# When weight pieces are converted in a fused attention and expert kernel, a third buffer of queries and keys, and when constant rows are written

## The chip, the cores and the metric

The kernel runs on one core of a Trainium2 chip. The metric is the device time of one execution in microseconds (us), given as the median of several runs.

## The reference

Three layers follow each other, all in float32; N = 2304 tokens (4 batches of 576), width 512.

```python
scores = 0.125 * q @ k.T           # 8 heads of 64; heads 0-3 a local mask of 32, heads 4-7 a strided one
attn = softmax(where(mask, scores, -1e9))
x = (attn @ v) -> (N, 512)
h = maximum(maximum(x @ w1, x @ w2), x @ w3)      # 512 -> 768
x = h @ w_out                                     # 768 -> 512
logits = x @ w_gate + modality_bias[modality_id]  # 8 experts, the largest logit chooses one
out[t] = gate[t] * (relu(x[t] @ w1[e]) @ w2[e])   # e = e(t); 512 -> 1024 -> 512
```

The weights w1, w2, w3 and w_out arrive as 64-bit words, and the kernel itself makes float32 of them.

## The kernel before

TensorE works on tokens in blocks of 384 (`TB`), six in all. For each block the function `L1(j, f)` computes the three products with w1, w2, w3 for one of six slices of 128 columns: three steps (m = 0, 1, 2) of 12 matmuls each, so 18 steps for a block. Each product is made of three matmuls, since every operand is held as a high and a low part. In the step with m = 0 ScalarE copies the bank of PSUM out, in the other two VectorE takes the maximum (L513). `L2(j)` is the product with w_out in six steps of 18 matmuls. A step takes the next bank by `mm_bank()`, which turns over two banks for as long as weights are being converted, and three later.

Attention is cut into 40 groups (batch, pair of heads, part), in the order of `order(b)`. One call of `slot()` is one slot: when it *ticks*, attention moves by one group through a pipeline of six stages (S of group t, maximum of t-1, exponential of t-2, reciprocal and product of t-3, transposition of t-4, product with v and its copy out of t-5). The matmul part of a slot ("rest", in `later`) is put out by `flush()`, in the middle of the next step of 12 matmuls. Ahead of block 0 stand 13 slots (t = 0 to 12) with no L1 step in them: there each slot is followed by four matmuls on constant data (`keep_warm(4)`, L861). I call these 13 slots the opening. After it, block 0's steps k = 1 to 18 each end in a slot; of these the odd ones up to 15 tick.

Conversion of a weight piece (24 pieces of 512 KB, 18 for w1 to w3 and 6 for w_out) also goes by slots, when `slot` is called with `conv`. It runs over three slots: `conv_abs` (ScalarE, L366), four VectorE operations of `conv_ops` (L378, L381, L383, L385, each needs the one before), and `conv_split` (ScalarE L397, POOL L398). Three stage buffers hold raw pieces, and the load of a further piece is asked for by `load_piece` right behind L385. The six pieces of w_out are followed by a transposition (`gate_T`, L405), which takes a bank by `mm_bank` as well, and a small product (`gate_G`, L411). Before, the opening converts from slot 4 on (`CS = 4`): nine of 13 slots. Block 0 converts in `pieces = 10 + 12 * k // 16`, so in all steps but k = 5, 9, 13 and 17; block 1 does what is left.

All loads stand in one queue, that of SP (SyncE), in the order of the program; one that waits holds up all behind it. Queries and keys of a pair of heads (608 KB) lie in one of two buffers, `qk_b[p % 2]`, and are asked for two slots ahead of the group that needs them (`load_qk(t + 2)`, L192). The scratch rows `xs`, into which POOL scatters the tokens by expert, are first filled with ones by eight DMAs from the tile `filler` (L902), in the steps k = 17 and 18 of block 0 and 1 to 6 of block 1. `L2(0)` stands behind five of the six slices of block 1. The outputs of L1 (`h_of`) lie in a ring of 11 chunks. The wide tile `y` is the buffer of three of four pieces in conversion; its first 72 columns hold the modality ids before that, from which POOL makes the bias table `ball` (L877 to L879) behind slot 1.

Of the kernel before, what the change touches and what calls it, by code (L numbers as in the profile page):

```python
# [106 lines left out]
def tile_attention_moe_moe(ctx: ExitStack, tc: tile.TileContext, qk, vw, w, wg, ids, bias, e12, cst, out):  # L107
# [7 lines left out]
    HT = sb.tile([128, 4608], F32R, name="HT")  # L115
    HX = sb.tile([128, 3072], F32R, name="HX")
    stage = sb.tile([128, 3, 2, 512], F32, name="stage")
# [24 lines left out]
    def f32(ap):  # L142
        return ap.bitcast(F32)
# [10 lines left out]
    spare = R[:, xo + 2 * KD * XR:xo + 2 * KD * XR + 768]  # L154
    chunks = [z[:, 768 * i:768 * i + 768] for z, n in ((HT, 6), (HX, 4)) for i in range(n)] + [spare]

    def h_of(j, f):
        return chunks[(NF * j + f) % 11].rearrange("p (s t) -> p s t", s=2)

    ht = [HT[:, 768 * i:768 * i + 768].rearrange("p (s t) -> p s t", s=2) for i in range(6)]  # L160
    ht2 = ht + [W[:, 16384 + 768 * i:16384 + 768 * i + 768].rearrange("p (s t) -> p s t", s=2) for i in range(2)]
    at_pool = tc.tile_pool(name="at", bufs=1)
    AT = at_pool.__enter__().tile([128, 5504], F32, name="AT")
    qk_b = [AT[:, 1216 * i:1216 * i + 1216].rearrange("p (s n) -> p s n", s=2) for i in range(2)]
    v_b = [AT[:, 2432 + 384 * i:2432 + 384 * i + 384].rearrange("p (c d) -> p c d", c=3) for i in range(3)]
    s_b = [AT[:, 3584 + 384 * i:3584 + 384 * i + 384] for i in range(3)]
    pt_b = [AT[:, 4736 + 384 * i:4736 + 384 * i + 384].rearrange("p (c q) -> p c q", c=3) for i in range(2)]

# [4 lines left out]

    filler = sb.tile([128, ROW // 2], F32R, name="filler")

# [11 lines left out]
    st = {}  # L187

    def load_qk(i):
        if i < NG and groups[i][2] == 0:  # L190
            b, p, _ = groups[i]
            SP.dma_start(qk_b[p % 2], qk[b, p])  # L192

# [31 lines left out]
    def att_S(i):  # L225
        b, p, g = groups[i]
        us, _ = units(p, g)
        t = qk_b[p % 2]
        ps, _, _, n, w_ = s_view(i)
# [121 lines left out]
    def load_piece():  # L351
        i = step["load"]
        if i < NW:
            step["load"] += 1
            SP.dma_start(stage[:, i % 3].rearrange("p a n -> p (a n)").bitcast(I32),
                         w[i].bitcast(I32))
# [63 lines left out]
    DEPTH = 5  # L420
    CS, FILL = 4, 16
    later, delayed, next_slot = [], [], []
# [5 lines left out]
    def slot(ticks=True, conv=True):  # L428
# [31 lines left out]
        def rest():  # L460
# [12 lines left out]
            if ticks:  # L473
                if t >= 2:
                    load_v(t - 2)
                if t:
                    load_qk(t + 2)

# [368 lines left out]
    with tc.manual_schedule():  # L847
# [15 lines left out]
        DVE.memset(t1s, 0.0)  # L863
        POOL.memset(AT[:, 3584:4736], 0.0)
        keep_warm(9)
        POOL.memset(f32(filler), 1.0)
        for t in range(LEAD + DEPTH):
            slot(conv=t >= CS)
            flush()
            keep_warm(4)  # L870
            if t == 1:
# [7 lines left out]
                POOL.tensor_tensor(out=ball, in0=ball, in1=other, op=ALU.add)  # L879
            if t == 2:  # L880
                for _ in range(3):
                    load_piece()

# [6 lines left out]
        for j in range(NB):  # L890
            parts = [(L1, j, f) for f in range(NF)]
            if j:
                parts.insert(NF - 1 if j == 1 else 1, (L2, j - 1))
            n = sum(3 if p_[0] is L1 else 2 * NS for p_ in parts) - 2
            start = now[0]
            k = 0
            for fn, *arg in parts:
                for _ in fn(*arg):
                    k += 1
                    if FILL <= fills < FILL + E:  # L900
                        e_ = fills - FILL
                        SP.dma_start(xs[NT * e_:NT * e_ + TB].rearrange("(p s) (h n) -> p (s h) n", p=128, h=2),  # L902
                                     f32(filler)[:, None, :].to_broadcast([128, 2 * NS, ROW // 2]))
                    fills += 1
                    due = goal.get(j, start)
                    pieces = 10 + 12 * k // 16 if j == 0 else NW + 3
                    slot(now[0] < min(due, start - (start - due) * k // n), fn is L1 and step["conv"] < pieces)
# [63 lines left out]
```

## Time and profile before

| | us |
|---|---|
| median of 3 runs | 640.86 |
| lowest, highest | 639.35, 643.72 |
| profiled execution, whole | 642.5 |
| its span from the first to the last instruction | 640.7 |
| outside the span | 1.8 |

The profile is of one execution. Its busy times and waits are those of the span; a time of a row counts from the span's start.

### The profile page before, as it was taken

The page shows a single profiled execution, that of the slowest core. Times are in us where ns is not written, and L with a number is a line of the kernel's source. Part 1 is how long each engine was busy: PE and PEld are TensorE (multiplying, and loading weights), DVE is VectorE, ACT ScalarE, POOL GpSimd, SP SyncE. Part 2 cuts the span into 40 slices and gives each one's busy share as a digit, 9 for nine tenths or more (in the row PEclk, how much of TensorE's full clock was granted, in tenths as well). Part 3 has the DMA queues.
Part 4 walks back from the last instruction along what each step waited for, and adds up shares of the span by engine and source line. Part 5 has one row for each costly group of instructions (what it writes and reads, how often), then busy time and mean ns, then how long its engine had stood idle before and what let it go on. Part 6 is the DMA issues. An engine that isn't in the chain of part 4 may idle for free. (4 is left out here: it accounts for less than half of the span.)

```text
span 640.7 us, 11895 instructions
## 1 busy us (share of the span) xinstructions
PE 612.7 (96%) x4597; PEld 563.6 (88%) x4603; DVE 258.2 (40%) x701; ACT 230.2 (36%) x695; POOL 136.1 (21%) x157
## 2 busy tenths in 40 slices
PE   7889998999999999999999999999999999999992
PEld 4558987899999999999999999998998979898981
DVE  4987996322334432442131123275344215331210
ACT  2868664333243334333211111352344124322220
POOL 2444553212131321032113103101102010111010
PEclk9979999999999999999999999999999999999997
DMA  6676459991022312020000004244442127220201
GB/s 229 228 274 211 160 189 234 178 161 44 22 74 63 108 55 65 23 78 10 10 18 34 1 1 145 86 134 136 160 133 86 47 75 243 83 67 33 68 19 40
DMA packets 30669, 64.45 MB, mean 101 GB/s; under 512 B 3328, under 2 KB 14336, under 8 KB 30592
## 3 DMA queue, kind: packets, MB, share of 16 engines
q1 hardware_dynamic: 27712, 54.01, 29.5%
q0 software_dynamic: 2880, 9.46, 3.9%
q8 instruction: 43, 0.70, 0.5%
q14 instruction: 34, 0.28, 0.1%
HBM read 47.68 MB, written 15.77 MB: 99 GB/s over the span
## 5 line engine op out<-in xcount | busy, mean ns | idle before, releaser
L494 PE MATMUL bank<-R,W 128*128 128x384 f32 (+1 forms) x1350 | 253.3, 343 | 3.3 <-DVE t1s L513 2.0
L494 PEld LDWEIGHTS bank<-R,W 128*128 128x128 f32 x1350 | 235.8, 188 | 9.5 <-DVE t1s L513 3.0
L494 PE MATMUL bank<-R,HT 128*128 128x260 f32 (+1 forms) x540 | 89.9, 316 | 0.3 <-POOL HT L505 0.3
L513 DVE TENSOR_TENSOR t1s<-bank,t1s 128x384 f32<-128x384 f32 x72 | 40.1, 557 | 122.5 <-PE bank L494 121.4
L494 PEld LDWEIGHTS bank<-R,HT 128*128 128x128 f32 x540 | 78.0, 188 | 6.8 <-POOL HT L505 0.5
L719 POOL DMA_INDIRECT out_dram<-y,gi x18 | 18.0, 1000 | 155.8 <-ACT x2h L700 99.0
L494 PE MATMUL bank<-x2h,R 128*128 128x384 f32 x192 | 49.5, 336 | 1.1 <-ACTq L927 1.1
L277 POOL TENSOR_TENSOR AT<-AT,mx 128x288 f32<-128x288 f32 (+2 forms) x40 | 27.1, 677 | 110.2 <-DVE mx L273 103.5
L494 PE MATMUL bank<-x2h,W 128*128 128x384 f32 x192 | 49.8, 337 | 0.0
L711 DVE SCALAR_TENSOR_TENSOR HT<-bank,HT 128x384 fp32r<-128x384 f32 x36 | 20.1, 557 | 63.1 <-ACT HT L710 62.9
L262 ACT ACTIVATE AT<-bank,mx 128x96 f32<-128x96 f32 (+1 forms) x138 | 43.1, 334 | 2.5 <-DVE R L415 1.7
L718 ACT ACTIVATE y<-bank,gi 128x512 f32<-128x512 f32 x18 | 12.4, 690 | 76.5 <-PE bank L494 63.1
L494 PE MATMUL bank<-W,HT 128*128 128x512 f32 x162 | 38.5, 391 | 0.0
L505 POOL TENSOR_TENSOR HT<-t1s,HT 128x384 fp32r<-128x384 f32 x21 | 21.3, 1014 | 73.5 <-ACT HT L504 73.4
L236 PE MATMUL bank<-AT 64*64 64x54 f32 (+1 forms) x640 | 32.0, 240 | 5.1 <-DMA AT<-in_qk_dram 4.4
L494 PEld LDWEIGHTS bank<-x2h,R 128*128 128x128 f32 x192 | 34.7, 188 | 1.6 <-ACTq L927 1.5
L494 PEld LDWEIGHTS bank<-W,HT 128*128 128x128 f32 x162 | 30.1, 188 | 6.0
L494 PEld LDWEIGHTS bank<-x2h,W 128*128 128x128 f32 x192 | 34.8, 188 | 0.3 <-issue 0.3
L236 PEld LDWEIGHTS bank<-AT 64*64 64x64 f32 x640 | 25.3, 139 | 11.1 <-DMA AT<-in_qk_dram 5.2
L710 ACT ACTIVATE HT<-bank 128x384 fp32r<-128x384 f32 x36 | 17.7, 492 | 47.0 <-PE bank L494 39.0
L343 DVE TENSOR_TENSOR R<-bank,R 128x162 fp32r<-128x162 f32 (+2 forms) x56 | 20.7, 397 | 32.3 <-ACT R L339 32.3
L511 ACT COPY t1s<-bank 128x384 f32<-128x384 f32 x36 | 17.3, 480 | 43.8 <-PE bank L494 39.0
(158 smaller groups left out, 803.3 us busy)
## 6 DMA issues: line engine op xcount, KB each, us to landing
stage<-in_w_dram SPq DMA_DIRECT2D x24, 512.0 KB, 4.2
stage<-in_e_dram SPq DMA_DIRECT2D x48, 256.0 KB, 3.3
AT<-in_qk_dram SPq DMA_DIRECT2D x15, 608.0 KB, 5.5
xs<-filler SPq DMA_DIRECT2D x8, 771.0 KB, 16.9
rows<-xs SPq DMA_DIRECT2D x7, 771.0 KB, 4.7
AT<-in_vw_dram SPq DMA_DIRECT2D x24, 144.0 KB, 3.6
AT<-in_vw_dram SPq DMA_DIRECT2D x16, 192.0 KB, 3.5
AT<-in_qk_dram SPq DMA_DIRECT2D x1, 352.0 KB, 5.2
```

The costliest lines, as they stand in the source:

```text
L236: PE.matmul(ps[r, c], lhsT=t[r, 0, q0:q0 + 64], rhs=t[r, 1, q0:q0 + w_], start=not pe, stop=True, skip_group_check=pe)
L262: ACT.activation(out=s3[:, c], in_=ps[:, c], func=AF.Exp, scale=0.125, bias=m[1][:, c:c + 1], accum_out=m[2][:, c:c + 1])
L277: POOL.tensor_tensor(out=s3, in0=s3, in1=m[3][:, :, None].to_broadcast([128, n, w_]), op=ALU.mult)
L343: DVE.tensor_tensor(out=l, in0=src, in1=f32(h), op=ALU.subtract)
L494: PE.matmul(ps, lhsT=a, rhs=b_, start=i == 0, stop=i == n - 1)
L505: POOL.tensor_tensor(out=h[:, 1], in0=t1, in1=f32(h[:, 0]), op=ALU.subtract)
L511: ACT.copy(t1, ps)
L513: DVE.tensor_tensor(out=t1, in0=ps, in1=t1, op=ALU.max)
L710: ACT.activation(out=h[:, 0], in_=ps, func=AF.Relu)
L711: DVE.scalar_tensor_tensor(out=h[:, 1], in0=ps, scalar=0.0, in1=f32(h[:, 0]), op0=ALU.max, op1=ALU.subtract)
L718: ACT.activation(out=y[:, s, :DM], in_=ps, func=AF.Copy, scale=gi[:, s, 0:1])
L719: POOL.indirect_dma_start(out=out[:, :], out_offset=bass.IndirectOffsetOnAxis(ap=gi[:, s, 1:2].bitcast(I32), axis=0), in_=y[:, s, :DM], in ...
```

## The change

Conversion begins at slot 2 of the opening and ends there with slot 8 (seven slots, pieces 0 to 6 begun), then goes on in each of the first 15 steps of block 0, pauses in steps 16 to 18 and finishes in block 1. The first three pieces are asked for behind slots 0, 1 and 2, one each. Queries and keys get a third buffer and are asked for three slots ahead. The eight fills start when the last piece has been asked for, one in every second step, each with rows of 514 elements where it had half rows of 257. `L2(0)` stands behind three slices of block 1, and the ring of chunks has 9.

```diff
-    HX = sb.tile([128, 3072], F32R, name="HX")
+    HX = sb.tile([128, 1536], F32R, name="HX")
...
-        return chunks[(NF * j + f) % 11].rearrange("p (s t) -> p s t", s=2)
+        return chunks[(NF * j + f) % 9].rearrange("p (s t) -> p s t", s=2)
...
-    AT = at_pool.__enter__().tile([128, 5504], F32, name="AT")
-    qk_b = [AT[:, 1216 * i:1216 * i + 1216].rearrange("p (s n) -> p s n", s=2) for i in range(2)]
+    AT = at_pool.__enter__().tile([128, 6720], F32, name="AT")
+    qk_b = [AT[:, 1216 * i:1216 * i + 1216].rearrange("p (s n) -> p s n", s=2) for i in range(3)]
...
-    filler = sb.tile([128, ROW // 2], F32R, name="filler")
+    filler = sb.tile([128, ROW], F32R, name="filler")
...
+    def qk_of(b, p):
+        return qk_b[(4 * b + (p + 2) % 4) % 3]
...
-            SP.dma_start(qk_b[p % 2], qk[b, p])
+            SP.dma_start(qk_of(b, p), qk[b, p])
...
-    CS, FILL = 4, 16
+    CS, AHEAD = 2, 7
...
-                    load_qk(t + 2)
+                    load_qk(t + 3)
...
-            slot(conv=t >= CS)
+            slot(conv=CS <= t < CS + AHEAD)
...
-            if t == 2:
-                for _ in range(3):
-                    load_piece()
+            if t < 3:
+                load_piece()
...
-                parts.insert(NF - 1 if j == 1 else 1, (L2, j - 1))
+                parts.insert(3 if j == 1 else 1, (L2, j - 1))
...
-                    if FILL <= fills < FILL + E:
-                        e_ = fills - FILL
-                        SP.dma_start(xs[NT * e_:NT * e_ + TB].rearrange("(p s) (h n) -> p (s h) n", p=128, h=2),
-                                     f32(filler)[:, None, :].to_broadcast([128, 2 * NS, ROW // 2]))
-                    fills += 1
+                    if step["load"] == NW and fills < 2 * E:
+                        if fills % 2 == 0:
+                            e_ = fills // 2
+                            SP.dma_start(xs[NT * e_:NT * e_ + TB].rearrange("(p s) n -> p s n", p=128),
+                                         f32(filler)[:, None, :].to_broadcast([128, NS, ROW]))
+                        fills += 1
...
-                    pieces = 10 + 12 * k // 16 if j == 0 else NW + 3
+                    pieces = min(AHEAD + k, 22) if j == 0 else NW + 3
```

VectorE in slots 9 and 10 of the opening, before. The mx rows and L244 are attention's, L378 to L385 are one piece in conversion, L343 is the copy out of an attention group.

```order
L269 TENSOR_SCALAR mx<-mx 128x3
L378 TENSOR_SCALAR y<-y 128x512
L273 RECIPROCAL mx<-mx 128x3
L381 TENSOR_SCALAR bank_82<-y 128x512
L244 TENSOR_REDUCE bank_83<-bank_83 128x3
L383 SCALAR_TENSOR_TENSOR bank_82<-stage,bank_82 128x512
L254 TENSOR_SCALAR mx<-bank_83 128x3
L385 SCALAR_TENSOR_TENSOR y<-stage,bank_82 128x512
L343 TENSOR_TENSOR R<-bank_86,R 128x192
```

The same place now; lines of the changed kernel are higher by three.

```order
L272 TENSOR_SCALAR mx<-mx 128x3
L276 RECIPROCAL mx<-mx 128x3
L247 TENSOR_REDUCE bank_83<-bank_83 128x3
L257 TENSOR_SCALAR mx<-bank_83 128x3
L346 TENSOR_TENSOR R<-bank_86,R 128x192
```

So the four operations of a piece have gone from there, as from slots 11 and 12; two of these four pieces now stand in slots 3 and 4, one more is in block 0 and one more in block 1.

VectorE in step 5 of block 0, before: a step that ticks, with no piece in it. L513 is the maximum of an L1 step.

```order
L513 TENSOR_TENSOR t1s<-bank_81,t1s 128x384
L269 TENSOR_SCALAR mx<-mx 128x6
L273 RECIPROCAL mx<-mx 128x6
L244 TENSOR_REDUCE bank_83<-bank_83 128x3
L254 TENSOR_SCALAR mx<-bank_83 128x3
L343 TENSOR_TENSOR R<-bank_86,R 128x9x18
L343 TENSOR_TENSOR R<-bank_87,R 128x9x18
L513 TENSOR_TENSOR t1s<-bank_80,t1s 128x384
```

The same step now.

```order
L516 TENSOR_TENSOR t1s<-bank_81,t1s 128x384
L272 TENSOR_SCALAR mx<-mx 128x6
L381 TENSOR_SCALAR y<-y 128x512
L276 RECIPROCAL mx<-mx 128x6
L384 TENSOR_SCALAR bank_82<-y 128x512
L247 TENSOR_REDUCE bank_83<-bank_83 128x3
L386 SCALAR_TENSOR_TENSOR bank_82<-stage,bank_82 128x512
L257 TENSOR_SCALAR mx<-bank_83 128x3
L388 SCALAR_TENSOR_TENSOR y<-stage,bank_82 128x512
L346 TENSOR_TENSOR R<-bank_86,R 128x9x18
L346 TENSOR_TENSOR R<-bank_87,R 128x9x18
L516 TENSOR_TENSOR t1s<-bank_80,t1s 128x384
```

A piece has come in between the two maxima, here and in steps 9 and 13; steps 16 and 18 have lost theirs.

SP's queue before, from the fifth weight piece asked for: `stage` is a weight piece, `AT` from `in_qk_dram` a load of queries and keys, from `in_vw_dram` one of values.

```order
L355 DMA stage<-in_w_dram 128x1024
L198 DMA AT<-in_vw_dram 96x384
L355 DMA stage<-in_w_dram 128x1024
L198 DMA AT<-in_vw_dram 96x384
L355 DMA stage<-in_w_dram 128x1024
L198 DMA AT<-in_vw_dram 96x384
L192 DMA AT<-in_qk_dram 128x1216
```

Now, from the seventh piece on:

```order
L358 DMA stage<-in_w_dram 128x1024
L201 DMA AT<-in_vw_dram 96x384
L358 DMA stage<-in_w_dram 128x1024
L201 DMA AT<-in_vw_dram 96x384
L195 DMA AT<-in_qk_dram 128x1216
L358 DMA stage<-in_w_dram 128x1024
L201 DMA AT<-in_vw_dram 96x384 x2
L195 DMA AT<-in_qk_dram 128x1216
```

The two loads of queries and keys at the end, for groups 10 and 12, stand one slot earlier, and behind the second the pieces of the slots 9 to 12 are gone.

## Rows read from the trace of the kernel before

**Rows 1.** The page's first part: busy time of each engine, share of span, instructions.

```profile
PE 612.7 (96%) x4597; PEld 563.6 (88%) x4603; DVE 258.2 (40%) x701; ACT 230.2 (36%) x695; POOL 136.1 (21%) x157
```

**Rows 2.** Timeline, TensorE, opening: start, duration, count, [idle before <- releaser].

```profile
28.52 1.04 PE L861 MATMUL bank<-t1s 128*128 128x512 bf16 x4
29.39 0.49 PE L286 MATMUL bank<-cs,AT 128*96 128x128 f32 x3
30.42 0.57 PE L313 MATMUL bank<-AT 96*64 96x64 f32 x12 [0.54 <-DVE R L343]
30.92 0.30 PE L232 MATMUL bank<-cs 128*128 128x288 bf16 x1
31.14 0.71 PE L236 MATMUL bank<-AT 64*64 64x96 f32 x12
...
36.53 1.53 PE L236 MATMUL bank<-AT 64*64 64x54 f32 x24 [2.28 <-DMA AT<-in_qk_dram]
...
46.27 3.52 PE L494 MATMUL bank<-R,W 128*128 128x384 f32 x18
```

**Rows 3.** Timeline, VectorE, opening: where slots 3, 6 and 9 begin.

```profile
10.85 0.49 DVE L268 TENSOR_REDUCE mx<-AT 128x6 f32<-128x324 f32 x1 [0.18 <-ACT AT L259]
...
19.77 0.42 DVE L268 TENSOR_REDUCE mx<-AT 128x5 f32<-128x270 f32 x1
...
30.49 0.16 DVE L269 TENSOR_SCALAR mx<-mx 128x3 f32<-128x3 f32 x1
```

**Rows 4.** Stretches: length, busy of each engine (instructions), granted clock, DMA share, GB/s.

```profile
10.85:19.77 8.92, 8.59 (x121) 5.58 (x122) 7.56 (x21) 4.25 (x15) 2.27 (x4) 1.00 1.00 360
36.00:41.00 5.00, 4.47 (x41) 2.95 (x43) 3.84 (x10) 2.70 (x10) 2.86 (x3) 0.50 0.91 305
46.30:92.80 46.50, 46.36 (x432) 42.27 (x430) 39.73 (x90) 32.26 (x114) 23.13 (x22) 1.00 0.59 194
```

**Rows 5.** Timeline, TensorE, end of block 0: waits for a bank.

```profile
93.70 0.66 PE L405 MATMUL bank<-cs,y 128*128 128x128 f32 x4 [0.86 <-DVE t1s L513]
...
97.89 1.31 PE L494 MATMUL bank<-R,W 128*128 128x384 f32 x6 [0.62 <-ACT t1s L511]
...
102.26 3.44 PE L494 MATMUL bank<-R,W 128*128 128x384 f32 x18 [0.72 <-DVE t1s L513]
```

**Rows 6.** Timeline, VectorE, block 0, steps 6 to 15.

```profile
65.27 0.56 DVE L513 TENSOR_TENSOR t1s<-bank,t1s 128x384 f32<-128x384 f32 x1 [0.55 <-PE bank L494]
...
68.59 0.16 DVE L269 TENSOR_SCALAR mx<-mx 128x5 f32<-128x5 f32 x1
...
72.03 0.54 DVE L513 TENSOR_TENSOR t1s<-bank,t1s 128x384 f32<-128x384 f32 x1
72.50 0.41 DVE L378 TENSOR_SCALAR y<-y 128x512 f32<-128x512 f32 x1
...
75.47 0.16 DVE L269 TENSOR_SCALAR mx<-mx 128x3 f32<-128x3 f32 x1
...
77.11 0.92 DVE L378 TENSOR_SCALAR w<-w 128x512 f32<-128x512 f32 x1
...
84.00 0.56 DVE L513 TENSOR_TENSOR t1s<-bank,t1s 128x384 f32<-128x384 f32 x1
...
89.71 0.56 DVE L513 TENSOR_TENSOR t1s<-bank,t1s 128x384 f32<-128x384 f32 x1 [1.08 <-PE bank L494]
...
93.09 0.55 DVE L513 TENSOR_TENSOR t1s<-bank,t1s 128x384 f32<-128x384 f32 x1
```

**Rows 7.** Timelines, POOL and ScalarE, opening: last bias operation, first Abs.

```profile
10.54 0.49 POOL L879 TENSOR_TENSOR ball<-ball,rt 128x144 f32<-128x144 f32 x1
...
14.91 0.67 ACT L366 ACTIVATE y<-stage 128x512 f32<-128x512 f32 x1 [1.30 <-DMA stage<-in_w_dram]
```

**Rows 8.** Timeline, SP: issue of the load that group 10 waits for.

```profile
30.93 0.42 SPq L192 DMA_DIRECT2D AT<-in_qk_dram  x1
```

**Rows 9.** Timeline, POOL, block 0: an operation that runs beside a piece's first step.

```profile
76.71 1.03 POOL L505 TENSOR_TENSOR HT<-t1s,HT 128x384 fp32r<-128x384 f32 x1
```

More of the change, by code (lines that the diff above doesn't have):

```diff
@@ L154, in tile_attention_moe_moe @@
     spare = R[:, xo + 2 * KD * XR:xo + 2 * KD * XR + 768]
-    chunks = [z[:, 768 * i:768 * i + 768] for z, n in ((HT, 6), (HX, 4)) for i in range(n)] + [spare]
+    chunks = [z[:, 768 * i:768 * i + 768] for z, n in ((HT, 6), (HX, 2)) for i in range(n)] + [spare]
     def h_of(j, f):
-        return chunks[(NF * j + f) % 11].rearrange("p (s t) -> p s t", s=2)
+        return chunks[(NF * j + f) % 9].rearrange("p (s t) -> p s t", s=2)
     ht = [HT[:, 768 * i:768 * i + 768].rearrange("p (s t) -> p s t", s=2) for i in range(6)]
@@ L162, in tile_attention_moe_moe @@
     at_pool = tc.tile_pool(name="at", bufs=1)
-    AT = at_pool.__enter__().tile([128, 5504], F32, name="AT")
-    qk_b = [AT[:, 1216 * i:1216 * i + 1216].rearrange("p (s n) -> p s n", s=2) for i in range(2)]
-    v_b = [AT[:, 2432 + 384 * i:2432 + 384 * i + 384].rearrange("p (c d) -> p c d", c=3) for i in range(3)]
-    s_b = [AT[:, 3584 + 384 * i:3584 + 384 * i + 384] for i in range(3)]
-    pt_b = [AT[:, 4736 + 384 * i:4736 + 384 * i + 384].rearrange("p (c q) -> p c q", c=3) for i in range(2)]
+    AT = at_pool.__enter__().tile([128, 6720], F32, name="AT")
+    qk_b = [AT[:, 1216 * i:1216 * i + 1216].rearrange("p (s n) -> p s n", s=2) for i in range(3)]
+    v_b = [AT[:, 3648 + 384 * i:3648 + 384 * i + 384].rearrange("p (c d) -> p c d", c=3) for i in range(3)]
+    s_b = [AT[:, 4800 + 384 * i:4800 + 384 * i + 384] for i in range(3)]
+    pt_b = [AT[:, 5952 + 384 * i:5952 + 384 * i + 384].rearrange("p (c q) -> p c q", c=3) for i in range(2)]
     ew = [
@@ L227, in att_S @@
         us, _ = units(p, g)
-        t = qk_b[p % 2]
+        t = qk_of(b, p)
         ps, _, _, n, w_ = s_view(i)
@@ L863, in tile_attention_moe_moe @@
         DVE.memset(t1s, 0.0)
-        POOL.memset(AT[:, 3584:4736], 0.0)
+        POOL.memset(AT[:, 4800:5952], 0.0)
         keep_warm(9)
```

## The prediction

> **What bounds the kernel now.** I read the busy times first. TensorE is busy for 612.7 of 640.7 us [rows 1]: whatever it does besides matmuls that must be done comes to 28 us and the constant matmuls of the opening. So a change that adds and removes no matmul can only move the moment at which block 0 begins, and the waits behind it. Next come stretches and timelines. In the opening TensorE waits for VectorE: its product with v starts only when VectorE has copied the last group out, at the end of its slot (0.54 us at 30.42), and slot 9 of VectorE begins at 30.49 [rows 2, 3]. The opening is thus as long as VectorE's slots, and the first L1 matmul comes at 46.27 [rows 2]. In block 0 it is turned round: up to 92.8 TensorE is busy for 46.36 of 46.50 us, and VectorE, with 39.73, has little to spare [rows 4]. At the end of block 0 TensorE waits three times for a bank, 0.86 + 0.62 + 0.72 = 2.2 us [rows 5]. One more thing in the opening: group 10 waits 2.28 us for its queries and keys, and the matmuls of 36 to 41 us run with a granted clock of 0.50, the lower level of 1.2 GHz [rows 2, 4].
>
> The sum is made on the profiled execution (642.5 us whole, 640.7 of it span), which took 1.6 us longer than the median of 640.86; what I find is then taken from the median.
>
> **The opening.** Prices first. A slot that ticks takes VectorE 72.03 - 68.59 = 3.44 us with a piece in it and 77.11 - 75.47 = 1.64 without [rows 6]. A piece costs about 1.7 us there (other slots of the two kinds lie nearer), less than its four operations alone, since attention's small ones fill its gaps.
>
> Slots 3 to 5 took 8.92 us from 10.85 to 19.77, with VectorE busy for 7.56 [rows 3, 4]. Slot 5 already has its piece; slots 3 and 4 now get one each: 7.56 + 2 x 1.7 = 10.96. In front of it the first Abs has to wait, since it writes into `y`, from which POOL reads the ids until 10.54 + 0.49 = 11.03; with 0.67 for the Abs it is done at 11.7, some 0.3 us after slot 3 wants it [rows 7]. Slot 6 then begins at 10.85 + 11.0 + 0.3 = 22.1. Slots 6 to 8 keep their pieces and their 30.49 - 19.77 = 10.72 us [rows 3], so slot 9 begins at 32.9, which is 2.4 us later than before.
>
> From there slots 9 to 12 have no piece. VectorE needs some 1.6 us for each, TensorE more: 0.87 for four constant matmuls, about 0.45 for the transposition, 0.5 for the product with v, and 0.25 + 0.65 to 0.85 for mask and scores [rows 2], so about 2.75 us. Three whole slots and, of slot 12, all but the transposition: 3 x 2.75 + 2.3 = 10.6. Block 0 begins at 32.9 + 10.6 = 43.5 instead of 46.27: **2.8 us gained**. The slots 9 to 12 were never seen without pieces. If chains between engines hold them to a converting slot's 3.4 us the gain is 0.8; at VectorE's 1.64 it would be past 5, but TensorE's work excludes more than 3.5.
>
> **Queries and keys.** The 2.8 us contain the end of the wait of 2.28 us. Before, the load was issued at 30.93 and the wait ended at 36.53, 5.6 us later [rows 2, 8]. Now it stands behind the eighth weight piece, which waits for the last operation of slot 7's piece: near 29.0, so the load goes out near 29.9 and lands at 35.5. S of group 10 comes at 32.9 + 2.75 + 0.75 = 36.4. It holds by 0.9 us. The other loads of this kind have more room.
>
> **Block 0.** TensorE's work is the same. VectorE gets a piece in steps 5, 9 and 13 too, 3 x 1.7 = 5.1 us up to step 15, and loses those of 16 and 18. It has slack to swallow: it waited for TensorE 0.55 us ahead of step 6's maximum and 1.08 ahead of step 14's [rows 6]; and its maximum of a step is wanted by TensorE only at the beginning of the step after next, since there are two banks. I follow it on the old clock, with block 0 where it was:
> - Step 12's maximum began at 84.00 without a wait. Two pieces more, less the 0.55: 86.85, done at 87.4. TensorE ends step 14 at 89.7, and a step with a tick takes it 12 matmuls of 0.187 and some 1.6 of attention, 3.85 [rows 2]; so step 14 began at 85.85 and now waits 1.55.
> - Step 14's maximum could have begun at 89.71 - 1.08 = 88.63; with three pieces more, less 0.55, 93.2, done at 93.7. In the middle of step 15 (89.7 + 1.55 + 1.1 = 92.35) the first transposition of a w_out piece wants that bank: 1.35 of waiting.
> - Step 15's maximum came 93.09 - 89.71 = 3.38 later: now 96.55, done at 97.1. TensorE ends step 15 at 93.7 + 0.5 + 1.1 = 95.3 and needs this bank for step 16: 1.8.
> - Behind the second transposition step 17 waits for ScalarE's copy, as before: 0.62 [rows 5].
>
> That is 5.3 us where there were 2.2: **3.1 us lost**. VectorE's catching up costs nothing, as steps 16 to 18 have no piece. The lower end: if a piece costs 0.3 less, the lag of nine or ten such steps shrinks by 1 to 2 us and the loss is near 1. The upper: nothing is swallowed, all of 5.1.
>
> A rule of the Trainium skill speaks against this part. The row: L378 takes 0.41 us at 72.50, and 0.92 at 77.11, where POOL's L505 runs from 76.71 to 77.74 [rows 6, 9]. The page SBUF — State Buffer (section SBUF: two separate sides) says that the one port pair which VectorE shares with GpSimd is an exclusive lock for a whole instruction, and that the loser blocks fully. The trace agrees. By that rule each of the three added pieces that meets a POOL operation would pay 0.5 us more, 1.5 in all, and the time would be 642.5; the sum below charges nothing for it, since the slots priced above had POOL beside them too.
>
> **The rest, each at nothing.** The last piece is asked for in step 15, where it was step 16 before, and the fills follow, spread over 14 steps. No wait of TensorE behind 46 us is put down to a load, and SP has no weight piece left to hold up, so faster or later fills gain nothing; the first scatter comes some five steps behind the last fill, and if it had to wait, POOL's products of queued groups would stand behind it for at most the few us of one fill. `L2(0)` moved forward does the same matmuls; it reads chunks 0 to 5 before slice 3 of block 1 writes them, so the ring of 9 adds no wait. Block 1 has four transpositions of w_out pieces before and after, with the same waits for banks. The `filler` memset is twice as long, ahead of all other work on POOL, which then waits for the ids anyway.
>
> **Sum:** -2.8 + 3.1 = +0.3, which is no more than its error. From the median: about **641.0 us**.
>
> **Rivals.**
> - *The gain stands.* VectorE's lag stays within the two banks, and the waits at the end of block 0 are the 2.2 us of before: 640.86 - 2.8 = 638.1. For it: the lag first passes the allowance in step 14, by 1.55 us, and if each of the ten converting slots up to there is shorter by 0.2 us, it doesn't. Against it: VectorE's 39.73 busy in 46.50 leave 6.8, and 5.1 are asked for.
> - *VectorE paces block 0.* The one that ends slower: from the fifth step on TensorE waits for every maximum, because the bank is handed back too late, and all of 5.1 us comes on top, with some 0.3 for locks: -2.8 + 5.4 = +2.6, 643.5. It decides from the point where a converting pair of steps takes VectorE longer than TensorE's 6.1; by rows it is 3.44 for a slot that ticks and 3.38 for a step that doesn't, with its maximum: 6.8 against 2.24 + 3.85 = 6.1 [rows 2, 6]. For it: that. Against it: the lag is zero at step 2 and needs ten steps to show.
> - *The load of group 10 is late all the same*, so the third buffer doesn't do what it is for. If the transfer takes 2 us longer than 5.6 TensorE waits 1.1 and perhaps runs slow behind it: the opening gains 1.3, and the sum is 642.7. For it: the DMA engines were full in slots 3 to 5 (share 1.00, 360 GB/s) [rows 4].
> - *The clock falls earlier.* Slots 3 to 5 now last some 3.7 us with 2 us of work for TensorE, so it stands still for 1.5 to 2 us in each; the 2.28 us wait was followed by 0.50. TensorE's 4.47 us of work at 0.50 would take some 2.2 at the upper level of 2.4 GHz [rows 4]; while VectorE sets the pace this costs nothing, and only a low clock in slots 9 to 12 would cost, about 2 us: 643.0. The page TensorE: Matmul & The Clock Gate (What's actually happening) states that the throttled state is the default and that activity releases it; the trace agrees as far as the one fall shows.
>
> **How the numbers follow.** Forecast 0.38, the gain stands 0.24, VectorE paces 0.14, late load 0.06, clock 0.06. The forecast's own range is 639.5 to 642.5. The range reaches to the gain with an opening that does still better by 1 us, 637.0, and to VectorE's pace with one of the small costs, 644.0. A measurement of this kernel can tell about 1 per cent, 6.4 us, from no change; none of the cases reaches that, so "within" has their 0.88. I leave 0.06 on the fast side for an opening shorter than TensorE's count allows, and 0.06 on the slow side for a scatter that waits for the fills or a conversion starved of loads.
>
> **What would show it.** Right: the first L1 matmul at 43 to 44 us; no wait for a load at group 10 and no 0.50 clock; TensorE waiting on t1s in steps 14 to 17 of block 0 for 4 to 6 us; the end of block 0 where it was, within 1 us. Wrong: a first L1 matmul above 45 or below 42, waits at the end of block 0 as small as before, or a new wait behind 130 us, where I expect the two traces alike.

## The result: 0.6 per cent slower, and the profile after

The changed kernel takes 644.76 us in the median of 11 runs (642.96 to 648.62), the kernel before 640.89 in 11 runs beside it (639.35 to 644.44). The ratio is 1.0059, 95% interval [1.0041, 1.0078]: some 3.8 us slower. The forecast was 641.0 with a range of 637.0 to 644.0, so the measurement lies outside, 0.8 us above its end. The nearest rival, "VectorE paces block 0", stood at 643.5. The interval leaves no doubt that the change costs time, though the prediction had said that a measurement could not tell less than 1 per cent from no change.

The profiled execution took 646.9 us, with a span of 645.1, against 642.5 and 640.7 before. Both are slower than their medians, by 2.1 us here and by 1.6 before. Lines of the changed kernel are higher by three (L494 is now L497, L378 is L381, and so on). The page's first part, beside [rows 1]:

```profile
PE 614.9 (95%) x4603; PEld 563.6 (87%) x4603; DVE 255.8 (40%) x701; ACT 230.0 (36%) x695; POOL 136.7 (21%) x157
```

No engine has more to do. Of the 4.4 us of the span, half are waits of TensorE; the other half is its longer busy time, 614.9 us instead of 612.7, for the same matmuls. Timeline of TensorE in the opening, beside [rows 2] (start, duration, operation, idle before):

```profile
7.93 1.79 PE L864 MATMUL bank<-t1s 128*128 128x512 bf16 x4
...
37.30 0.91 PE L239 MATMUL bank<-AT 64*64 64x54 f32 x24
...
44.53 3.51 PE L497 MATMUL bank<-R,W 128*128 128x384 f32 x18
```

and of VectorE, where slots 3, 6 and 9 begin, beside [rows 3]:

```profile
12.08 0.48 DVE L271 TENSOR_REDUCE mx<-AT 128x6 f32<-128x324 f32 x1
...
23.24 0.42 DVE L271 TENSOR_REDUCE mx<-AT 128x5 f32<-128x270 f32 x1
...
33.95 0.17 DVE L272 TENSOR_SCALAR mx<-mx 128x3 f32<-128x3 f32 x1
```

Group 10 no longer waits for its queries and keys (0.91 us at 37.30, where there were 1.53 behind a wait of 2.28), and block 0 begins at 44.53 instead of 46.27: 1.74 us earlier, not 2.8. Slots 3 to 5 took 11.16 us (forecast 11.0), slots 6 to 8 10.71 (10.72), slots 9 to 12 10.58 (10.6). Only slot 3 was misplaced: it begins at 12.08 where 11.15 was counted. Four constant matmuls that take 1.04 elsewhere took 1.79 at 7.93, behind a wait of TensorE of 1.52 us; the granted clock (TensorE's clock as a share of its full one) is 0.89 in the first 16 us, and 0.50 from 9 to 11 us.

The end of block 0 on TensorE, beside [rows 5]:

```profile
85.79 1.32 PE L497 MATMUL bank<-R,W 128*128 128x384 f32 x6 [0.85 <-DVE t1s L516]
...
89.92 0.37 PE L235 MATMUL bank<-cs 128*128 128x288 bf16 x1 [1.99 <-ACT AT L265]
90.22 1.23 PE L239 MATMUL bank<-AT 64*64 64x96 f32 x12
91.38 3.28 PE L497 MATMUL bank<-R,W 128*128 128x384 f32 x12
...
97.56 1.31 PE L497 MATMUL bank<-R,W 128*128 128x384 f32 x6 [1.42 <-DVE t1s L516]
```

ScalarE ahead of the longest of these waits:

```profile
86.92 0.68 ACT L369 ACTIVATE y<-stage 128x512 f32<-128x512 f32 x1 [2.87 <-DMA stage<-in_w_dram]
...
88.79 0.35 ACT L265 ACTIVATE AT<-bank,mx 128x96 f32<-128x96 f32 x1
```

The load of that weight piece, on VectorE and in SP's queue (the row of SP holds two issues, the first at 81.49):

```profile
80.73 0.69 DVE L388 SCALAR_TENSOR_TENSOR w<-stage,bank 128x512 int32<-128x512 int32 x1
81.49 3.60 SPq L358 DMA_DIRECT2D stage<-in_w_dram  x2
```

VectorE in the same place, and an operation of POOL beside it:

```profile
85.18 0.55 DVE L516 TENSOR_TENSOR t1s<-bank,t1s 128x384 f32<-128x384 f32 x1
...
88.24 1.50 DVE L381 TENSOR_SCALAR y<-y 128x512 f32<-128x512 f32 x1
...
88.18 1.27 POOL L401 TENSOR_TENSOR W<-y,W 128x512 fp32r<-128x512 f32 x1 [3.66 <-ACT W L400]
```

And the stretches of 16 us that hold it (length, busy time of TensorE, its weight loads, VectorE, ScalarE, POOL, then TensorE's granted clock, DMA share, GB/s):

```profile
62.00:78.00 16.00, 15.79 (x146) 13.88 (x143) 15.58 (x37) 12.24 (x37) 9.48 (x10) 1.00 0.55 187
78.00:94.00 16.00, 13.03 (x108) 11.32 (x107) 14.56 (x32) 10.25 (x30) 9.21 (x9) 0.89 0.60 202
```

A stretch of the kernel before, for comparison:

```profile
64.00:80.00 16.00, 16.00 (x146) 14.93 (x147) 15.01 (x33) 10.95 (x38) 8.31 (x9) 1.00 0.49 161
```

In [rows 4] TensorE was busy for 46.36 of 46.50 us of block 0; here VectorE comes first, busy for 15.58 of 16 us, and then TensorE loses 3 us in the next 16. The busy share of VectorE decides nothing by itself: it was 15.01 of 16 us in the kernel before, where TensorE stood still for none of them. The waits of 0.85 and 1.42 us are of the predicted kind (a maximum too late to free the bank). The wait of 1.99 us is of another: the exponentials (L265) stand on ScalarE behind an Abs (L369) that waited 2.87 us for its weight piece, whose load went out at 81.49, when VectorE's L388 was done, and landed 5.4 us later. Behind it the scores took 1.23 us (0.71 elsewhere) and 12 matmuls 3.28 (2.25 elsewhere), with a granted clock of 0.89 in this stretch and 0.50 from 90 to 93 us: 1.5 us more.

Two marks on TensorE divide the spans: the first L1 matmul, and the 13th attention transposition behind it (in block 1, past all conversion). Before: 46.27 to the first, 129.70 between them, 464.7 from there to the end. After: 44.53, 136.07, 464.5. So the opening gave 1.7 us, block 0 and the first part of block 1 took 6.4, and all the rest, 464 us with the fills and the scatter, is the same. The prediction had 2.8 and 3.1.

VectorE's last maximum of block 0, that of step 18, before and after, parts the 6.4 us:

```profile
104.68 0.56 DVE L513 TENSOR_TENSOR t1s<-bank,t1s 128x384 f32<-128x384 f32 x1 [2.40 <-PE bank L494]
108.23 0.56 DVE L516 TENSOR_TENSOR t1s<-bank,t1s 128x384 f32<-128x384 f32 x1 [1.61 <-PE bank L497]
```

Counted from the first L1 matmul it comes after 58.41 us before and 63.70 now: 5.3 us are lost in block 0, and 1.1 in block 1.

### The profile page after: what moved, and what is told of

It is laid out like the page before. It is cut to its first block, busy times and chain, and to the rows that moved or that the text cites. A ratio compares the mean times of both kernels' runs of the same rounds, so it can differ in the third digit from the quotient of the medians.

```text
span 645.1 us, 11885 instructions
## 1 busy us (share of the span) xinstructions
PE 614.9 (95%) x4603; PEld 563.6 (87%) x4603; DVE 255.8 (40%) x701; ACT 230.0 (36%) x695; POOL 136.7 (21%) x157
## 5 line engine op out<-in xcount | busy, mean ns | idle before, releaser
L497 PE MATMUL bank<-R,W 128*128 128x384 f32 (+1 forms) x1350 | 255.2, 344 | 5.6 <-DVE t1s L516 4.2
L497 PEld LDWEIGHTS bank<-R,W 128*128 128x128 f32 x1350 | 236.4, 189 | 13.2 <-DVE t1s L516 6.7
L497 PE MATMUL bank<-R,HT 128*128 128x260 f32 (+1 forms) x594 | 95.4, 313 | 0.0
L497 PEld LDWEIGHTS bank<-R,HT 128*128 128x128 f32 x594 | 84.0, 188 | 6.4
L497 PE MATMUL bank<-x2h,R 128*128 128x384 f32 x192 | 49.5, 336 | 1.1 <-ACTq L930 1.1
L497 PE MATMUL bank<-x2h,W 128*128 128x384 f32 x192 | 49.8, 337 | 0.0
L265 ACT ACTIVATE AT<-bank,mx 128x96 f32<-128x96 f32 (+1 forms) x138 | 43.0, 332 | 2.1 <-DVE R L418 1.7
L497 PE MATMUL bank<-W,HT 128*128 128x512 f32 x162 | 38.5, 391 | 0.0
L497 PEld LDWEIGHTS bank<-x2h,R 128*128 128x128 f32 x192 | 34.7, 188 | 1.6 <-ACTq L930 1.5
L497 PEld LDWEIGHTS bank<-W,HT 128*128 128x128 f32 x162 | 30.1, 188 | 5.9
L497 PEld LDWEIGHTS bank<-x2h,W 128*128 128x128 f32 x192 | 34.8, 188 | 0.3 <-issue 0.3
L508 POOL TENSOR_TENSOR HT<-t1s,HT 128x384 fp32r<-128x384 f32 x24 | 24.6, 1025 | 49.3 <-ACT HT L507 49.1
L239 PEld LDWEIGHTS bank<-AT 64*64 64x64 f32 x640 | 25.2, 138 | 10.8 <-issue 5.6
L497 PE MATMUL bank<-x2l,R 128*128 128x384 f32 x96 | 32.3, 336 | 0.0
```

The costliest lines, as they stand in the source:

```text
L239: PE.matmul(ps[r, c], lhsT=t[r, 0, q0:q0 + 64], rhs=t[r, 1, q0:q0 + w_], start=not pe, stop=True, skip_group_check=pe)
L265: ACT.activation(out=s3[:, c], in_=ps[:, c], func=AF.Exp, scale=0.125, bias=m[1][:, c:c + 1], accum_out=m[2][:, c:c + 1])
L497: PE.matmul(ps, lhsT=a, rhs=b_, start=i == 0, stop=i == n - 1)
L508: POOL.tensor_tensor(out=h[:, 1], in0=t1, in1=f32(h[:, 0]), op=ALU.subtract)
```

## The experiments

Two theories stood after the result for those 6.4 us. **Loads:** the weight pieces land late, ScalarE waits for them, and the exponentials queue behind. **VectorE's work:** the three pieces added to steps 5, 9 and 13 use up its slack, and late loads are what this looks like on ScalarE. Beside them: what did the third buffer and the seven early slots do by themselves? The kernel "before" ran beside every batch (641.6, 641.0 and 641.3 us). The table has the ratio to it, and the marks of one profiled execution.

| kernel | us | ratio [95%] | first L1 | to the 13th | rest |
|---|---|---|---|---|---|
| after | 644.76 | 1.0059 [1.0041, 1.0078] | 44.53 | 136.07 | 464.5 |
| e1 | 646.29 | 1.0068 [1.0046, 1.0089] | 44.57 | 135.59 | 464.4 |
| e2 | 640.79 | 0.9988 [0.9973, 1.0003] | 45.27 | 129.74 | 463.8 |
| e3 | 650.71 | 1.0160 [1.0131, 1.0189] | 50.16 | 134.25 | 464.5 |
| e4 | 638.08 | 0.9945 [0.9926, 0.9964] | 43.24 | 129.04 | 463.9 |
| e5 | 642.31 | 1.0020 [1.0000, 1.0039] | 46.08 | 132.99 | 463.8 |
| e6 | 640.4 | 1.0008 [0.9974, 1.0041] | 44.95 | 129.02 | 463.9 |
| e7 | 643.76 | 1.0049 [1.0022, 1.0075] | 41.18 | 133.44 | 464.0 |
| e8 | 639.77 | 0.9981 [0.9961, 1.0002] | 42.51 | 132.57 | 464.4 |
| e9 | 638.79 | 0.9973 [0.9949, 0.9997] | 41.64 | 131.56 | 464.4 |
| e10 | 643.12 | 1.0048 [1.0028, 1.0068] | 42.25 | 134.94 | 464.0 |
| e11 | 642.54 | 1.0042 [1.0009, 1.0074] | 43.39 | 132.36 | 463.9 |
| e12 (e4 again) | 639.08 | 0.9956 [0.9937, 0.9975] | 44.12 | 129.82 | 464.0 |

The last column hardly moves: what any of these edits does is done by the 13th mark. The marks are those of one execution each: the first L1 matmul of one and the same kernel scatters by about 0.9 us (e4, e12), and e5, whose opening differs from theirs by one memset, has it 2 to 3 us later.

**e1: a fourth stage buffer.** The changed kernel, with weight pieces asked for one piece earlier (room made by a ring of 8 chunks, `L2(0)` behind two slices, fills of half rows).

```diff
-    stage = sb.tile([128, 3, 2, 512], F32, name="stage")
+    stage = sb.tile([128, 4, 2, 512], F32, name="stage")
...
-            if t < 3:
+            if t < 4:
                 load_piece()
```

> The changed kernel with a fourth stage buffer for weight pieces, so that each load is asked for one piece earlier (room for it: ring of 8 chunks, L2(0) behind two slices, filler of half rows). Theory A, loads late: in block 0 an Abs waits for its piece in ScalarE's queue (up to 2.87 us in the changed kernel) and attention's exponentials stand behind it; with a piece asked for a step earlier these waits go, and with them TensorE's wait of 1.99 us for ScalarE at 89.9 us and the low clock behind it: about 4 us less than the changed kernel, 640 to 641.5. Theory B, VectorE's work: the three added pieces make VectorE late by themselves; the waits for t1s in steps 14 to 16 (0.85 and 1.42 us and what the low clock hides) stay and the time stays within 1 us of the changed kernel, 644.

In block 0 ScalarE no longer waits for a weight piece at all, and the time is that of the changed kernel. TensorE's waits in block 0 are now all of the other kind:

```profile
72.60 1.32 PE L497 MATMUL bank<-R,W 128*128 128x384 f32 x6 [0.77 <-DVE t1s L516]
86.91 1.33 PE L497 MATMUL bank<-R,W 128*128 128x384 f32 x6 [1.49 <-DVE t1s L516]
93.91 0.66 PE L408 MATMUL bank<-cs,y 128*128 128x128 f32 x4 [1.66 <-DVE t1s L516]
96.89 1.32 PE L497 MATMUL bank<-R,W 128*128 128x384 f32 x6 [1.27 <-DVE t1s L516]
```

The loads' theory falls as the main cause: to the 13th mark it is 135.59, 0.5 us better than the changed kernel. That the wait of 1.99 us was only the form that VectorE's lateness took there is likely, but not shown, as the edit also moved the ring, the fills and `L2(0)`. The last three of these waits, in steps 14, 15 and 16, are those that the prediction counted: 1.49, 1.66 and 1.27 us, where it had 1.55, 1.35 and 1.8.

**e2: the old pace.** The changed kernel with nine slots of the opening (2 to 10) and block 0 in three steps of four.

```diff
-    CS, AHEAD = 2, 7
+    CS, AHEAD = 2, 9
...
-                    pieces = min(AHEAD + k, 22) if j == 0 else NW + 3
+                    pieces = 10 + 12 * k // 16 if j == 0 else NW + 3
```

> The changed kernel with nine converting slots in the opening (2 to 10) and block 0 paced as before (no piece in steps 5, 9, 13, 17). Theories A and B alike: the loss in block 0 goes, TensorE's waits there are near the 2.2 us of before, and block 0 begins about 1.4 us later than in the changed kernel, near 46; 640 to 641. Theory C, that the rest of the change costs (fills spread over 14 steps, L2(0) moved, ring of 9): within 1 us of the changed kernel, 644.

640.79 us. Block 0 begins at 45.27, only 0.7 us later than in the changed kernel, where 1.4 was expected. The waits at the end of block 0 are near those of [rows 5] again (0.60, 0.62 and 0.72), and it is 129.74 to the 13th mark where the kernel before has 129.70. Against the changed kernel that is 0.71 per cent, 4.5 us.

**e3: the pace alone,** in the kernel before (`CS, AHEAD = 2, 7`, one piece asked for behind each of slots 0 to 2, `pieces = min(AHEAD + k, 22)`; two buffers of queries and keys, the old fills and ring).

> The kernel before with the conversion's new pace alone (slots 2 to 8, every step of block 0 up to 15, first pieces asked for one by one); two buffers of queries and keys, fills and L2(0) as before. Theories A and B: the loss of some 6 us in block 0 and its neighbours is there, and the opening gains less than 1.7 us as the wait of group 10 may stay: 644 to 647. Theory C: 640 to 641.

650.71 us, more than the 644 to 647 expected. The part behind the opening is there (134.25). The opening, which was expected to gain a little, is 3.9 us longer: with two buffers the load of group 10 still stands behind slot 8, which two pieces more have put back, so it goes out at 34.02 instead of 30.93 [rows 8], and TensorE waits longer:

```profile
40.78 1.53 PE L236 MATMUL bank<-AT 64*64 64x54 f32 x24 [3.71 <-DMA AT<-in_qk_dram]
```

**e4: all but the pace.** The changed kernel with the old pace in the opening too: slots 4 to 12, the first three pieces asked for behind slot 2.

```diff
-    CS, AHEAD = 2, 7
+    CS, AHEAD = 4, 9
...
-            if t < 3:
-                load_piece()
+            if t == 2:
+                for _ in range(3):
+                    load_piece()
...
-                    pieces = min(AHEAD + k, 22) if j == 0 else NW + 3
+                    pieces = 10 + 12 * k // 16 if j == 0 else NW + 3
```

> The changed kernel with the conversion's pace of before (slots 4 to 12, no piece in steps 5, 9, 13, 17, three pieces asked for behind slot 2): third buffer of queries and keys, fills, ring and L2(0) as changed. Theories A and B: the wait of group 10 (2.28 us) and the low clock behind it go, nothing else moves: 638 to 639. Theory C: 643 to 645.

638.08 us, faster than both kernels, and again 0.9956 on another chip (e12, below). TensorE, opening and end of block 0:

```profile
36.53 0.50 PE L289 MATMUL bank<-cs,AT 128*96 128x128 f32 x3 [1.28 <-ACT AT L302]
...
41.49 0.30 PE L235 MATMUL bank<-cs 128*128 128x324 bf16 x1 [1.07 <-ACT AT L265]
...
43.24 3.52 PE L497 MATMUL bank<-R,W 128*128 128x384 f32 x18
...
90.47 0.66 PE L408 MATMUL bank<-cs,y 128*128 128x128 f32 x4 [0.66 <-DVE t1s L516]
```

Nine converting slots end at 43.24, no later than the changed kernel's seven. VectorE's slots tell why. The operation L272, near the start of slots 3, 6 and 9 in e4, and of slots 3 and 6 in the changed kernel:

```profile
11.73 0.18 DVE L272 TENSOR_SCALAR mx<-mx 128x6 f32<-128x6 f32 x1
...
19.11 0.17 DVE L272 TENSOR_SCALAR mx<-mx 128x5 f32<-128x5 f32 x1
...
29.36 0.16 DVE L272 TENSOR_SCALAR mx<-mx 128x3 f32<-128x3 f32 x1
```

```profile
12.59 0.17 DVE L272 TENSOR_SCALAR mx<-mx 128x6 f32<-128x6 f32 x1
...
23.69 0.17 DVE L272 TENSOR_SCALAR mx<-mx 128x5 f32<-128x5 f32 x1
```

From slot 3 to slot 6 e4 takes 19.11 - 11.73 = 7.4 us, with one piece, against 23.69 - 12.59 = 11.1 in the changed kernel, with three: 1.9 us for each of the two. Slot 9 begins at 29.36, and from there to block 0 are 13.9 us with four pieces, against 33.95 to 44.53, 10.6 us, with none: 0.8 for each, of which waits for ScalarE (1.28 and 1.07) are more than half.

**e5: VectorE's work alone.** e4, with the four kinds of operation of a piece on scratch data in steps 5, 9 and 13 of block 0: no load, no Abs, no split, and they change no result.

```diff
+        DVE.tensor_scalar(out=gate_t, in0=gate_t, scalar1=LEAST, scalar2=MOST, op0=ALU.max, op1=ALU.min)
+        yield
+        DVE.tensor_scalar(out=wps, in0=g, scalar1=3, scalar2=0x3FFFFFF8, op0=ALU.logical_shift_left, op1=ALU.bitwise_and)
...
+                    extra[0] = j == 0 and k in (5, 9, 13)
```

> The kernel of e4_all_but_pace with four VectorE operations on a scratch tile, of a piece's kinds and shapes, put into the steps 5, 9 and 13 of block 0: VectorE's part of the three added pieces without their loads, Abs, casts or POOL work; nothing that is used is computed by them. Theory B, VectorE's work: block 0 loses what it loses in the changed kernel, 4 to 6 us, 642 to 644. Theory A, loads and ScalarE's queue: within 1 us of e4, 638 to 639.

1.0020 against 0.9945 for e4 on another chip: 0.75 per cent, 4.8 us (the medians are 4.2 apart), of which the marks give 132.99 - 129.04 = 4.0 between them. VectorE is full, with 39.38 of 40 us where e4 has 36.57 in the same place, and TensorE waits for its maxima:

```profile
60.00:100.00 40.00, 36.28 (x358) 31.77 (x358) 39.38 (x90) 24.82 (x83) 18.75 (x19) 1.00 0.53 176
```

```profile
87.60 1.32 PE L510 MATMUL bank<-R,W 128*128 128x384 f32 x6 [1.46 <-DVE t1s L529]
...
97.27 0.66 PE L421 MATMUL bank<-cs,y 128*128 128x128 f32 x4 [1.66 <-DVE t1s L529]
```

Up to the last maximum of block 0 it takes 62.19 us, where e4 takes 58.22 and the changed kernel 63.70. So three pieces' worth of VectorE work, with nothing else, brings back 4.0 of the 5.5 us that the changed kernel loses there against e4. This shows the second theory, which e1 only left standing. (The profiled execution is the slowest of the ten. What it has beyond this against e4 lies in the opening, where four constant matmuls at 12.10 us took 1.89.)

**e6: two buffers of queries and keys.** e4 with `qk_b[p % 2]` and `load_qk(t + 2)`.

> The kernel of e4_all_but_pace with two buffers of queries and keys and loads two slots ahead again; what is left of the change is fills, ring and L2(0). If the third buffer carries the gain of e4: group 10 waits for its load again and the time is that of the kernel before, 640.5 to 642. If fills, ring or L2(0) carry it: 638 to 639.

1.0008, where e4 has 0.9945 and 0.9956: by these ratios the third buffer is worth 0.5 to 0.6 per cent, 3.3 to 4.0 us, give or take 2.5. The medians themselves lie 1.3 to 2.3 us apart and the first marks 0.8 to 1.7, so there is a gain, but its size is uncertain, 1 to 4 us. What is left of the change without it and without the pace (fills, ring, `L2(0)`) is 0.5 us with an interval of 2 us to either side. Its opening has the wait back:

```profile
36.28 0.91 PE L239 MATMUL bank<-AT 64*64 64x54 f32 x24 [2.46 <-DMA AT<-in_qk_dram]
```

**e7: seven slots, but late.** The changed kernel with `CS, AHEAD = 6, 7` (slots 6 to 12).

> The changed kernel with its seven converting slots at 6 to 12 of the opening instead of 2 to 8; block 0 as changed. Theory O, place: a piece costs the opening 1.7 us where VectorE sets the pace (slots 3 to 6) and next to nothing in slots 9 to 12, where TensorE's own work takes 2.8 us a slot; block 0 begins near 40, and the time is 4 to 5 us below the changed kernel, 640 to 641. Rival, number: what counts is that seven slots convert, block 0 begins at 44 to 45 and the time is 644 to 645.

The opening does what was expected: first L1 matmul at 41.18, 3.35 us earlier than with slots 2 to 8, for the same seven pieces. The time does not: its executions reach from 640.68 to 647.22, with a median of 643.76, near the rival's 644 to 645. The profiled one was the fastest, so its marks don't show where the others lose. The three slowest have granted clocks of 0.987 to 0.989 over the whole span, the fastest 0.995, but one of 645.15 us has 0.994; how the executions differ stays open.

**e8: one piece fewer in e4's opening.** `CS, AHEAD = 5, 8` and `pieces = 9 + 12 * k // 16`.

> The kernel of e4_all_but_pace with eight converting slots, 5 to 12, block 0 with pieces = 9 + 12 * k // 16, one piece more in block 1. Theory O: slot 5 is 1.7 us shorter and the piece costs some 0.6 in block 1: 636.5 to 637.5. Rival: the piece costs in block 1 what it saves, 638 to 639.

First L1 matmul 0.7 us earlier than in e4, and 3.5 us more from there to the 13th mark: 639.77 us, 0.9981. That is slower than either theory had it: the piece left to block 1 cost more than it saved.

**e9: e4 with a fourth stage buffer,** as in e1, four pieces asked for behind slot 2.

> The kernel of e4_all_but_pace (third buffer, new fills, old pace) with a fourth stage buffer, so that a weight piece is asked for one piece earlier (room made by a ring of 8 chunks, L2(0) behind two slices of block 1 and fills of half rows). In e4 TensorE's two waits of 1.28 and 1.07 us in the opening (L289 and L235 behind ScalarE) stood behind an Abs that waited for its piece. Theory 'the loads still cost the opening': both go, the first L1 matmul comes near 42 us instead of 43.24, and the time is near 637. Rival 'VectorE sets the slots of the opening and the load waits lie beside it': first L1 matmul within 0.4 us of 43.2, time 638.1 within 0.7.

One of the two waits in the opening goes (the other stays at 1.08 us), block 0 begins at 41.64, and the time is no better than e4's on the same chip (638.79 against 639.08; by the ratios it is 0.2 per cent worse). It gives back 2.5 us between the marks, partly in a stretch from 100 to 120 us with a granted clock of 0.91. So still earlier loads bring no gain that these runs can see; whether the ring of 8 or the place of `L2(0)` takes part in that was not tried apart.

**e10: block 0's pace alone,** in e4.

```diff
-                    pieces = 10 + 12 * k // 16 if j == 0 else NW + 3
+                    pieces = min(9 + k, 22) if j == 0 else NW + 3
```

> The kernel of e4_all_but_pace with one edit: block 0 converts in every step from 1 to 13 (pieces 9 + k, then a pause) instead of three steps in four; the opening keeps its nine slots 4 to 12. Theory 'VectorE's work in block 0' (as the changed kernel adds it): TensorE waits on t1s in steps 13 to 16, first L1 matmul near 43.2 as in e4, and the time is 4 to 5.5 us above e4: 642 to 643.5. Rival 'the loads, which the early start of the changed kernel left late': here the loads run with the same lead as in e4, so the time is within 1.5 us of e4, 638 to 639.5. Rival 'the pause afterwards gives it back': below 640.

643.12 against 639.08 us for e4's kernel on the same chip: 4.0 us, 0.9 per cent by the ratios. Between the marks it is 134.94 against 129.82. The longest wait is for VectorE, at the first transposition of a w_out piece, which stands in step 13 here:

```profile
85.23 0.66 PE L408 MATMUL bank<-cs,y 128*128 128x128 f32 x4 [1.81 <-DVE t1s L516]
```

The pause in steps 14 to 18 does not give it back: VectorE's maximum of step 18 comes 62.50 us behind the first L1 matmul, 4.3 later than in e4.

**e11: the early opening alone,** block 0 at three steps of four, with two pieces more left to block 1 than in e4.

```diff
-                    pieces = min(AHEAD + k, 22) if j == 0 else NW + 3
+                    pieces = 8 + 12 * k // 16 if j == 0 else NW + 3
```

> The changed kernel with one edit: block 0 converts in three steps of four (pieces 8 + 12 k // 16); the opening keeps its seven slots 2 to 8, and two pieces more are left to block 1. Theory (the early slots cost 1.3 us in the opening, the added pieces of block 0 some 5.4): first L1 matmul near 44.5, waits at the end of block 0 as small as in the kernel before, and the time 1 to 2 us above e4: 639 to 640.5. Rival 'the early start is what costs, through the loads and the clock': the time stays at 643.5 or above. If the two pieces more in block 1 cost VectorE's pace there, it is between, near 642.

642.54 us, the third of the expected cases. Block 0 has lost nothing (its seventh transposition comes 40.29 us behind the first L1 matmul, as in the kernel before, where the changed kernel has 42.42), and the opening ends at 43.39, as e4's does. But the two pieces that it has not converted cost 3.3 us in block 1. There each step with a transposition of a w_out piece waits some 0.65 us for a bank, and this pace has more such steps; behind the last one the matmuls run slower, 6.87 us for 30 that took 5.55 in e4, and the stretch shows 0.91:

```profile
125.43 1.31 PE L497 MATMUL bank<-R,W 128*128 128x384 f32 x6 [0.65 <-DVE t1s L516]
127.37 1.06 PE L414 MATMUL bank<-wgt,gate_t 128*128 128x8 f32 x8 [0.63 <-ACT AT L265]
...
130.25 6.87 PE L497 MATMUL bank<-R,W 128*128 128x384 f32 x30
```

```profile
120.00:140.00 20.00, 18.07 (x136) 16.76 (x135) 4.11 (x13) 5.83 (x23) 3.98 (x4) 0.91 0.49 135
```

**e12: e4 once more,** on another chip.

> The kernel of e4_all_but_pace once more, on another chip, beside the three others. If its gain is real: 0.993 to 0.997 of the kernel before, 637 to 639 us; first L1 matmul near 43.2. If it was that chip's: 0.998 to 1.001.

0.9956 [0.9937, 0.9975]: the gain over the kernel before is real, some 2.8 us by the ratio.

## Why the prediction was wrong

Four of the kernels make a way from before to after in steps, by their ratios (each difference is uncertain by 1.5 to 2.5 us). e6, with the fills, the ring and `L2(0)` alone: +0.5 us. e4, with the third buffer: -4.0. e2, with the nine slots put two earlier: +2.8. The changed kernel, with seven of them and a piece in every step of block 0: +4.5. The steps add up to the measured +3.8 by construction, so their sum proves nothing; what counts is which of them are large.

**What bounds the kernel** was read rightly: the opening is as long as VectorE's slots where they convert, and behind the 13th mark nothing moved. One new wait stands behind 130 us, though (0.70 at 135.60, below), where the prediction expected the two traces alike.

**The opening.** The time of its end was nearly right: 43.5 forecast; 44.53, 44.57 (e1) and 43.39 (e11) in three executions. The prices and the slots held (7.56 + 3.4 for slots 3 to 5, 2.75 for a slot without a piece); the miss of 0.9 us in the profiled execution is the slower clock at 7.93 us, which e11 did not have. But of the 2.8 us, 2.28 were the wait for queries and keys and 0.5 were credited to moving pieces out of slots 9 to 12. That credit was wrong. It compared with slots that waited for loads. With the third buffer those slots cost little for their pieces (0.8 us each in e4, against 1.9 in slots 3 and 4), since TensorE has 2.75 us of work in them anyway. Put into slots 2 to 10, the same nine pieces lose 2.8 us (e2). And seven early pieces end the opening no sooner than nine late ones (e11, e4), while the two that are left out must be paid for later.

**Queries and keys.** Right: the wait is gone, the margin was enough, and e6 shows that the third buffer carries the gain of e4, within some 2 us. The rival "late all the same" is excluded.

**The step that failed is the loss behind the opening,** "3.1 us lost": four waits at the end of block 0 and nothing in block 1. It measured 6.4 us, of which 5.3 in block 0 and 1.1 in block 1. The prediction's own sign, the end of block 0 "where it was, within 1 us", missed too: it came 3.55 us later.

In block 0 the mechanism was the forecast one, VectorE's lag of three pieces, and e5 and e10 show it by itself (4 to 6 us). The four waits of the sum came to 0.85, 0, 1.42 and 0.57 us in the profiled execution, 2.8 where 5.3 were counted. Three things stood in their place that the sum did not have:

- The lag shows before step 14. VectorE's maximum of step 6, right behind the first added piece, comes 1.6 us later than before, and TensorE loses 0.4 us up to step 8 (the 24 matmuls from 62.17 take 4.86 us, where they took 4.48) and 1.3 ahead of its wait in step 14. The sum had let the lag stay harmless up to there.
- VectorE's lateness also holds back the next load (`load_piece` stands behind L388), so ScalarE's Abs, so the exponentials queued behind it: 1.99 us.
- The slower matmuls behind that wait: 1.5 us.

How these share the loss differs from run to run, so in part the size is one execution's. Here are the kernels with that pace in block 0, then three without it (us from the first L1 matmul to the last maximum of block 0, and from there to the 13th mark):

| kernel | block 0 | from there |
|---|---|---|
| after | 63.70 | 72.37 |
| e1 | 63.00 | 72.59 |
| e3 | 61.36 | 72.89 |
| e7 | 61.04 | 72.40 |
| e10 | 62.50 | 72.44 |
| before | 58.41 | 71.29 |
| e4 | 58.22 | 70.82 |
| e2 | 58.94 | 70.80 |

In e3 and e7 block 0 loses 3.0 and 2.6 us, as forecast; in e1, where no load was late, the counted waits came nearly as counted, and with the earlier drift and one wait more (0.77 at 72.60) the loss was 4.6.

**Block 1** was put at nothing, with "the same waits for banks", and this term is wrong in every run: the pace leaves a piece more to block 1, and the five kernels with it take some 1.6 us more there (e3 against before, where `L2(0)` stands in its old place; the others against e2 and e4). From the last maximum of block 0 to the 13th mark TensorE waits four times before, 2.1 us, and six times now, 3.8 us, which is that difference. The last two are these:

```profile
129.74 1.32 PE L497 MATMUL bank<-R,W 128*128 128x384 f32 x6 [0.65 <-DVE t1s L516]
...
135.60 0.91 PE L239 MATMUL bank<-AT 64*64 64x54 f32 x24 [0.70 <-ACT AT L265]
```

The earlier `L2(0)` gives back 0.5 us of it (71.29 against 70.8).

**The rivals.** "VectorE paces block 0" came nearest by its number and had the rows for it (6.8 us asked in 6.1), but not by its mechanism: it had TensorE wait for every maximum from the fifth step on, and the timeline of the changed kernel shows no wait of that kind before step 14, at 85.79. "Needs ten steps to show" was still a poor reason against it, since the lag shows at step 6. That its 643.5 lies near 644.76 is partly luck, as it had no loss in block 1 and a gain of 2.8 in the opening.

**The price of the lock.** VectorE's L381 took 1.50 us at 88.24, where it takes 0.42 alone; POOL's L401 ran from 88.18 to 89.45. That agrees with the Trainium skill, SBUF — State Buffer (section SBUF: two separate sides), which the prediction weighed at 1.5 us in all and left out. What it cost in sum no run here tells apart: e5's scratch operations met POOL too.

**The rest at nothing.** For the fills, the ring and `L2(0)` e6 bears it out within 2 us.

## What to carry to other kernels

Moving work off one stage is worth what that stage's bound engine saves, less what the receiving stage has no slack for: price it at both ends, per place (here a piece cost 0.8 us in slots where TensorE has work of its own, 1.9 where VectorE sets the pace, 1.3 to 1.6 in block 0, where VectorE was busy for 85 per cent, and 1.6 in block 1, which the prediction had left out). When two engines are both near full, a lag doesn't stay inside the buffers; count it from the first step, and follow it through the queues that hang on the late engine, loads asked for behind it above all. And before a change with several parts is accepted or rejected, time the parts: here one part gained 1 to 4 us and another lost 7.

## What the runs showed of the hardware

The granted clock fell to 0.50 in places where it had not before, behind waits of TensorE: 1.79 us instead of 1.04 for four constant matmuls behind a wait of 1.52 us (and likewise behind 1.60 in e1), and 3.28 instead of 2.25 for 12 matmuls behind one of 1.99. The length of the wait alone does not tell it. A wait of 1.29 us at the first of these places, in the kernel before, had no such sequel, nor had waits of 1.66 us in e1 and e5 and of 1.81 in e10 at the end of block 0. The fall need not come at once either: at group 10 the kernel before was at 0.50 when its wait of 2.28 us ended (1.53 us for 24 matmuls), while in e6, behind 2.46 us, the same matmuls took 0.91 and the four constant ones after them 1.78. A forecast can only carry such a fall as a spread, here an estimated 1 to 2 us for each (0.9 and 1.5 in the changed kernel).

The fills landed in 8.1 us in the median, where they took 16.9 before, with a DMA share of 0.60 instead of 1.08 from 100 to 120 us. The whole rows are the smaller part of that: e1 and e9, which kept half rows but have the new spacing, took 10.8 and 11.2. No time hung on it here.
